# All four ds tiles of a block by DMA transpose, and the plain transfers on GpSimd's queue, from step 160 of an attention backward

## The chip, the cores and the metric

The kernel runs on one core of a Trainium2 chip. The metric is the device time of one execution in microseconds (us); lower is better. The median of the kernel before was 1445.82 us in three runs (1442.79 to 1448.91, a spread of 0.4%) when the prediction was made. The names of the engines in the profile are PE (TensorE), PEld (TensorE's weight loads), DVE (VectorE), ACT (ScalarE), POOL (GpSimd) and SP (SyncE, which here does little but issue DMAs).

## The reference

The kernel computes one transformer block and all its gradients: the output and the gradients of `x`, `wqkv`, `wo` and the three feed-forward weights.

```python
# S = 2048 positions, D = 448, H = 16 heads of 28, F = 1792; bf16 inputs
def attention(x, wqkv, wo):
    q, k, v = split_heads(x @ wqkv)
    p = softmax((q @ k.T) * 28 ** -0.5)
    return merge_heads(p @ v) @ wo

def feed_forward(x, w_gate, w_up, w_down):
    return (silu(x @ w_gate) * (x @ w_up)) @ w_down

def forward(x, ...):
    xn = layernorm(x)
    return x + attention(xn, wqkv, wo) + feed_forward(xn, w_gate, w_up, w_down)

# outputs: forward(...) and its vjp at grad_out
```

The change lies in the backward pass of the attention. For each pair of heads and each pair of a key range and a query range the kernel makes the gradient of the scores, `ds` = (dp product from TensorE) x exp(scores). The gradient of q needs `ds` with keys on the partitions, so every tile of `ds` is transposed into `dsT`.

## The kernel before

The backward has 512 steps. Four steps (`qi` = 0 to 3) are one "block", 128 blocks in all. A step makes one `ds` tile of 128 x 1024 in bf16 (two heads side by side). In a block three tiles are transposed by DMA from SyncE's queue, and the fourth (`qi` = 3) by eight TensorE transposes into PSUM and one ScalarE copy out of it.

```python
def dst_dma(b, ds, qi):
    if qi == 0:
        dsT[b] = bk.tile([P, 4, 2, 4, P], BF16, name="dsT", bufs=3)
    SP.dma_start_transpose(out=dsT[b][:, qi].rearrange("p j kt s -> p (j kt) s"),
                           in_=ds[:].rearrange("p j k -> p (j k)"))

def ew(k):                                   # elementwise work of a step
    ...                                      # ScalarE: exp of the scores into e_sb
        ds = dss[k - 1] = kq.tile([P, 2, 512], BF16, name="ds_sb", bufs=10)
        for j in range(2):
            DVE.tensor_tensor(out=ds[:, j], in0=dps.pop((k - 1, j))[:], in1=est[k - 1][:, j], op=ALU.mult)
        if qi < 2 or qi == 2 and b < NB // 4 - 1:
            ...                              # dst_dma(b, ds, qi)

def tr_unit(b):
    for qi in (3,) if b < NB // 4 - 1 else (2, 3):
        ds = dss.pop(4 * b + qi)
        ps = ps_b.tile([P, 8, P], BF16, name="db", bufs=3)
        for c in range(8):
            PE.transpose(ps[:, c, :], ds[:, c // 4, (c % 4) * P:(c % 4 + 1) * P], ident_bf[:])
        o = dsT[b][:, qi].rearrange("p j kt s -> p (j kt) s")
        ...                                  # qi 2: VectorE copies
            ACTE.copy(out=o, in_=ps[:])      # qi 3
```

`dq_unit(b)` is the reader: 16 matmuls on `dsT`, about nine steps after the block's last `ds`. Beside this, the kernel brings in the data of later work in plain DMA loads of 0.25 to 0.5 MB. A rate rule spreads them over the steps ("drip"), and they go out from SyncE's queue, between the transposes. Results are stored from GpSimd's queue (`store`).

```python
def drop():                                  # called once a step
    ...
    while slow and credit > 0:
        _, _, o, i = slow.pop(0)
        SP.dma_start(out=o, in_=i)
        credit -= size(o)

def load_dx(ch, fq):                         # the largest stream of loads: dau_c, 14 of the 31 MB after step 160
    ...
    d = dxs["pool"].tile([P, 5, 2, 512], BF16, name="dau_c")
    drip(("dx", ch, fq), [(d[:, i - f0:min(i + 2, f1) - f0], F_d[ch, :, i:min(i + 2, f1), 1:3, :]) for i in range(f0, f1, 2)], now + 16)
```

The softmax here doesn't subtract the row's maximum and nothing guards it: scores larger than these inputs give would overflow.

Of the kernel before, what the change touches and what calls it, by code (L numbers as in the profile page):

```python
# [11 lines left out]
FP32 = mybir.dt.float32  # L12
# [91 lines left out]
def kernel(  # L104
# [23 lines left out]
    PE, DVE, ACTE, POOL, SP = nc.tensor, nc.vector, nc.scalar, nc.gpsimd, nc.sync  # L128
# [419 lines left out]
    for i in range(len(chain) + LEAD):  # L548
# [4 lines left out]
        k = i - LEAD  # L553
        if k >= 0:
            b = chain[k]
# [98 lines left out]
    for t in range(4):  # L654
        run(T_unit(xnT, xn_t, t, t % 2 == 0, ps_s if t < 2 else None))
    DVE.tensor_reduce(out=r_ones[:],
                      in_=ident_f[:].rearrange("p (a b) -> p a b", b=HP)[:, :, 28:30],
# [11 lines left out]
    for c in range(3):  # L669
        k = 4 * c  # L670
# [72 lines left out]
    now = 0  # L743
# [13 lines left out]
    def drop():  # L757
        nonlocal credit
        if not slow:
            credit = 0  # L760
            return
        rate, cum = RATE, 0
        for due, _, o, _ in slow:
            cum += size(o)
            rate = max(rate, (cum - credit) / max(due - now - 3, 1))
        credit += rate
        while slow and credit > 0:
            _, _, o, i = slow.pop(0)
            SP.dma_start(out=o, in_=i)
            credit -= size(o)  # L770

    def have(*keys):
        for x in [x for x in slow if x[1] in keys]:
            slow.remove(x)
            SP.dma_start(out=x[2], in_=x[3])

    def load_q(g, qc):
        t = new_q(g, qc)
# [8 lines left out]
    NB = len(steps)  # L787
    dqT, dkv, acc, dsT = {}, {}, {}, {}
    est, dss, sps, dps = {}, {}, {}, {}
# [32 lines left out]
                dps[k - 1, j] = d_ps  # L822

    bk, pend = None, []

    def dst_dma(b, ds, qi):
        if qi == 0:
# [4 lines left out]
    def ew(k):  # L832
        if k < NB:
            est[k] = kq.tile([P, 2, 512], BF16, name="e_sb", bufs=5)
            for j in range(2):
                ACTE.activation(out=est[k][:, j], in_=sps.pop((k, j))[:], func=ACT.Exp, scale=SCALE)  # L836
        if 1 <= k <= NB:
            g, hp, kc, qc, qi = steps[k - 1]
            b = (k - 1) // 4
            ds = dss[k - 1] = kq.tile([P, 2, 512], BF16, name="ds_sb", bufs=10)  # L840
            for j in range(2):
                DVE.tensor_tensor(out=ds[:, j], in0=dps.pop((k - 1, j))[:], in1=est[k - 1][:, j], op=ALU.mult)  # L842
            if qi < 2 or qi == 2 and b < NB // 4 - 1:
                if bk is None:
                    pend.append(lambda: dst_dma(b, ds, qi))
                else:
                    dst_dma(b, ds, qi)
# [9 lines left out]
    k = n = 0  # L857
# [10 lines left out]
    bk = bwd.enter_context(tc.tile_pool(name="bk", bufs=2, reuse_waits="tile"))  # L868
# [7 lines left out]
    def late_dw(c):  # L876
# [10 lines left out]
            store(o[d0:d0 + dn, F - P:], w2[:dn, c, a])  # L887
        yield 110

    dq_acc = bk.tile([P, S // 2], FP32, name="dq_acc", bufs=1)  # L890

    def tr_unit(b):
        for qi in (3,) if b < NB // 4 - 1 else (2, 3):
            ds = dss.pop(4 * b + qi)
            ps = ps_b.tile([P, 8, P], BF16, name="db", bufs=3)
            for c in range(8):
                PE.transpose(ps[:, c, :], ds[:, c // 4, (c % 4) * P:(c % 4 + 1) * P], ident_bf[:])  # L897
            o = dsT[b][:, qi].rearrange("p j kt s -> p (j kt) s")
            if qi == 2:
                DVE.tensor_copy(out=o, in_=ps[:])  # L900
            else:
                ACTE.copy(out=o, in_=ps[:])  # L902

    def kv(k):
        g, hp, kc, qc, qi = steps[k]
        first, last = (qc == 0 and qi == 0), (qc == 3 and qi == 3)
        if first:
            acc[0] = ps_g.tile([P, 512], FP32, name="acc")
        a = acc[0]
        e = est.pop(k)  # L910
        ds = dss[k] if qi == 3 or k == NB - 2 else dss.pop(k)
        sp4 = qside[g, qc][:, 2:4, qi * P:(qi + 1) * P]
        for j in range(2):
            r = HP * pv(2 * hp + j)
            PE.matmul(a[r:r + HP, :], lhsT=sp4[:, 1, r:r + HP], rhs=e[:, j, :],  # L915
                      start=first, stop=last, tile_position=(0, r), skip_group_check=True)
        for j in range(2):
            r = HP * (2 * hp + j)
            PE.matmul(a[r:r + HP, :], lhsT=sp4[:, 0, r:r + HP], rhs=ds[:, j, :],  # L919
                      start=first, stop=last, tile_position=(0, r), skip_group_check=True)  # L920
        if last:
            if kc == 0:
                need(lambda: g == 0 or (g - 1, hp + 1, 1) in s_done)
                dkv[g, hp] = bk.tile([P, S], BF16, name=f"dkv{hp}", bufs=1)
            ACTE.activation(out=dkv[g, hp][:, kc * 512:(kc + 1) * 512], in_=a[:], func=ACT.Copy,
                            scale=(sc_a if hp == 0 else sc_b)[:, 0:1])
            if g < G - 1:
                ksl = slice(kc * 512, (kc + 1) * 512)
                store(dqkvT_d[3 * g + 1 + hp, :, ksl], dkv[g, hp][:, ksl])
            if kc == 3:  # L930
                if g < G - 1:
                    push(*[(480, lambda t8=t8: dsp_unit(g, hp + 1, t8)) for t8 in range(2)])
                elif hp == 0:
                    push(*[(480, lambda t8=t8: dsp_unit(g, hp + 1, t8)) for t8 in range(2)])

    def dq_unit(b):
        g, hp, kc, qc, _ = steps[4 * b]
        t = dsT.pop(b)
        ks = kside[g, kc][:, 2, :].rearrange("p (t r) -> p t r", r=P)
        ps = ps_g.tile([P, 512], FP32, name="genb")  # L940
        for kt in range(4):
            for par in range(2):
                for j in range(2):
                    r = HP * (2 * par + j)
                    h = HP * (2 * hp + j)
                    PE.matmul(ps[r:r + HP, :256], lhsT=ks[:, kt, h:h + HP], rhs=t[:, par::2, j, kt, :],  # L946
                              start=(kt == 0), stop=(kt == 3), tile_position=(0, r), skip_group_check=True)
        qsl = slice(qc * 256, (qc + 1) * 256)
        if kc == 0:
            ACTE.mul(out=dq_acc[:, qsl], in_=ps[:, :256], mul=SCALE)  # L950
            return
        if kc == 3 and hp == 0 and qc == 0:
            dqT[g] = bk.tile([P, 2, S // 2], BF16, name="dqT", bufs=1)
        if kc == 3 and g == G - 1:
            DVE.scalar_tensor_tensor(out=dqT[g][:, hp, qsl], in0=ps[:, :256], scalar=SCALE, in1=dq_acc[:, qsl],  # L955
                                     op0=ALU.mult, op1=ALU.add)
            return
        st = bk.tile([P, 256], FP32, name="dq_st", bufs=1)
        ACTE.mul(out=st[:], in_=ps[:, :256], mul=SCALE)  # L959
        if kc < 3:  # L960
            POOL.tensor_tensor(out=dq_acc[:, qsl], in0=dq_acc[:, qsl], in1=st[:], op=ALU.add)  # L961
            return
        POOL.tensor_tensor(out=dqT[g][:, hp, qsl], in0=dq_acc[:, qsl], in1=st[:], op=ALU.add)
        if qc == 3:
            dst = dqkvT_d[3 * g].rearrange("r (a q s) -> r a q s", q=2, s=P)
            for par in range(2):
                store(dst[64 * hp:64 * hp + 64, :, par],
                      dqT[g][64 * par:64 * par + 64, hp].rearrange("r (a s) -> r a s", s=P))
            if hp == 1:
                stream[3:3] = [(480, lambda hp=hp: dsq_unit(g, hp)) for hp in range(2)]  # L970
                at = [i for i, u in enumerate(stream) if u[1] in (dx_open, tail_open)]
                at = max(at[0] + 1, 5) if at and g != 1 else 5
                s_done.add((g, "w"))
                stream[at:at] = [(2590, lambda c=c: dwq_unit(g, c)) for c in range(4)]

    def dsq_unit(g, hp, tag="genb"):
        ps = (ps_b if tag == "rest" else ps_g).tile([P, 8, P], BF16, name=tag, bufs=2 if tag == "rest" else 1)
        for j in range(8):
            PE.transpose(ps[:, j, :], dqT[g][:, hp, j * P:(j + 1) * P], ident_bf[:])
            if j < 7:  # L980
                yield 60
        DVE.tensor_copy(out=dsp[g][:, :, 0, 64 * hp:64 * hp + 64],
                        in_=ps[:].rearrange("p a (q x) -> p (a q) x", q=2))
        yield 60


    dsp = {}

    def dsp_unit(g, kind, t8, tag="genb"):
# [6 lines left out]
        for j in range(8):  # L996
            t = 8 * t8 + j
            PE.transpose(ps[:, j, :], src[:, t * P:(t + 1) * P], ident_bf[:])
            if j < 7:
                yield 60  # L1000
        (ACTE.copy if tag == "rest" and t8 else DVE.tensor_copy)(out=dsp[g][:, 8 * t8:8 * t8 + 8, kind, :], in_=ps[:])
        s_done.add((g, kind, t8))
        yield 60

# [2 lines left out]
    def dwq_unit(g, c, tag="genb"):  # L1007
# [6 lines left out]
                yield 162  # L1014
        o = bk.tile([P, 3, 4, DH], BF16, name="dwq_o")
        p4 = ps[:].rearrange("p (k h r) -> p k h r", k=3, r=HP)
        cp = ACTE.copy if tag == "rest" else DVE.tensor_copy
        cp(out=o[:dn, 0], in_=p4[:dn, 0, :, :DH])
        cp(out=o[:dn, 1:3, 0:2, :], in_=p4[:dn, 1, :, :DH].rearrange("p (k h) r -> p k h r", k=2))
        cp(out=o[:dn, 2, 2:4, :], in_=p4[:dn, 2, 0:2, :DH])  # L1020
# [364 lines left out]
```

## Time and profile before

| kernel before | value | from |
|---|---|---|
| span of the profiled run, granted clock | 1440.1 us, 0.985 | spans by core |
| TensorE, VectorE, ScalarE busy, whole span | 92%, 80%, 88% | overview |
| block 40 to block 120, from the first `ds` of each | 486.3 us, 6.08 us a block | starts in the trace |
| in those 80 blocks: TensorE, VectorE, ScalarE busy | 467, 443, 446 us | records of the trace |
| SyncE inside DMA issues in the same 80 blocks | 433 us | records of the trace |
| plain traffic in the 80 blocks: SyncE's queue, GpSimd's queue | 30.8 MB, 4.4 MB | packet records |

The table is to be read against the 486 us: TensorE is at 96% of them, and of the others SyncE has the most left, 11%. An engine's busy share doesn't say which resource sets the pace here. The lines of the views are in the prediction below.

### The profile page before, as it was taken

To read this page: it belongs to the slowest core of one execution; us is meant where nothing else is said; L and a number is where in the kernel's file an instruction comes from. 1 tells how busy PE (TensorE), PEld (TensorE's weight loads), DVE (VectorE), ACT (ScalarE), POOL (GpSimd) and SP (SyncE) were. 2 spreads that over 40 slices of the span, in tenths; PEclk is the share of its full clock that TensorE was granted. 3 is DMA by queue.
4 is the path that set the end of the run, shared out by engine and by line. 5 is a ranking of instruction groups with operands and counts; after the bars stand their busy time and mean duration, and the time that the engine had idled before them with its cause. 6 is when DMAs were issued, how large, how long until landed. Compare 5 with 4: busy or idle time off the path is not lost. (4 is left out here: it accounts for less than half of the span.)

```text
span 1440.1 us, 34682 instructions
## 1 busy us (share of the span) xinstructions
PE 1326.3 (92%) x12647; PEld 541.0 (38%) x12708; DVE 1151.8 (80%) x1997; ACT 1261.5 (88%) x2193; POOL 403.6 (28%) x561
## 2 busy tenths in 40 slices
PE   5889999999999999889999999999999999999996
PEld 2333333333333333333333434433443444444343
DVE  6667757666676676578998998888889999989988
ACT  5789988988889999869989989899989999989974
POOL 6464524464334454111112112201111011010006
PEclk9999999999999999989999999999999999999998
DMA  5796956796678586799999999999999999999971
GB/s 154 181 199 165 235 122 160 187 195 164 146 162 192 147 172 145 178 234 226 226 213 217 232 220 188 196 209 229 228 173 194 209 223 230 201 191 203 198 142 60
DMA packets 681179, 271.69 MB, mean 189 GB/s; under 512 B 606424, under 2 KB 655824, under 8 KB 681008
## 3 DMA queue, kind: packets, MB, share of 16 engines
q1 hardware_dynamic: 672576, 255.35, 87.1%
q0 software_dynamic: 7024, 13.82, 4.1%
q8 instruction: 100, 1.64, 0.5%
q14 instruction: 71, 0.58, 0.1%
q10 hardware_dynamic: 1408, 0.30, 0.1%
HBM read 65.09 MB, written 60.36 MB: 87 GB/s over the span
## 5 line engine op out<-in xcount | busy, mean ns | idle before, releaser
L842 DVE TENSOR_TENSOR ds_sb<-db,e_sb 128x512 bf16<-128x512 f32 x1024 | 646.8, 684 | 51.3 <-issue 21.1
L836 ACT ACTIVATE e_sb<-sb 128x512 bf16<-128x512 f32 x1024 | 554.8, 611 | 60.4 <-PE db L820 44.5
L612 ACT ACTIVATE eT<-s_w 128x1024 bf16<-128x1024 f32 x256 | 263.5, 1029 | 46.1 <-PE s_ps L609 43.1
L614 ACT ACTIVATE eT<-s_ps 128x512 bf16<-128x512 f32 x512 | 280.4, 612 | 0.0
L820 PE MATMUL db<-kd,qd 32*128 32x512 bf16 x1024 | 234.4, 384 | 8.2 <-DVE ds_sb L842 7.4
L812 PE MATMUL sb<-kd,qd 32*128 32x512 bf16 x1024 | 210.4, 387 | 5.1 <-DMA qd<-QD_d 3.3
L961 POOL TENSOR_TENSOR dq_acc<-dq_acc,dq_st 128x256 f32<-128x256 f32 x64 | 46.2, 721 | 455.4 <-ACT dq_st L959 455.4
L919 PE MATMUL acc<-ds_sb,qd 128*32 128x512 bf16 x1024 | 161.0, 391 | 0.0
L915 PE MATMUL acc<-e_sb,qd 128*32 128x512 bf16 x1024 | 158.8, 391 | 1.3 <-DVE dw_o L528 1.3
L902 ACT COPY dsT<-db 128x1024 bf16<-128x1024 bf16 x128 | 130.1, 1016 | 14.6 <-PE db L897 13.9
L380 POOL TENSOR_TENSOR nn<-nn,ag 128x512 f32<-128x512 f32 x56 | 71.2, 1271 | 252.2 <-DVE ag L378 243.7
L609 PE MATMUL s_ps<-QQ,KK 32*128 32x512 bf16 x512 | 125.4, 385 | 3.9
L1128 PE MATMUL genb<-wguT,dau_c 128*128 128x448 bf16 x448 | 117.5, 355 | 6.3 <-ACT dq_st L959 3.9
L609 PE MATMUL s_w<-QQ,KK 32*128 32x512 bf16 x512 | 100.3, 387 | 13.1 <-ACT eT L612 10.4
L812 PEld LDWEIGHTS <-qd 32*128 32x128 bf16 x1024 | 48.2, 91 | 149.4 <-issue 140.3
L421 PE MATMUL gen<-xn_t,f_sp 128*128 128x448 bf16 x416 | 91.8, 354 | 2.6 <-DVE nn L395 1.7
L421 PEld LDWEIGHTS <-f_sp 128*128 128x128 bf16 x640 | 55.7, 98 | 75.0 <-issue 31.9
L946 PE MATMUL genb<-dsT,kd 128*32 128x256 bf16 x2048 | 79.5, 275 | 1.9 <-DVE dqT L955 0.6
L897 PE MATMUL db<-ident_bf,ds_sb 128*128 128x128 bf16 x1032 | 79.4, 220 | 1.1 <-DVE ds_sb L842 1.1
L897 PEld LDWEIGHTS <-ds_sb 128*128 128x128 bf16 x1032 | 68.3, 99 | 24.1 <-issue 5.3
L451 PE MATMUL gen<-eT,VS 128*32 128x512 bf16 x1024 | 68.4, 384 | 5.5 <-DVE nn L395 3.3
L381 POOL TENSOR_TENSOR nn<-nn,tt 128x512 f32<-128x512 f32 x56 | 72.0, 1286 | 4.4
(167 smaller groups left out, 1911.0 us busy)
## 6 DMA issues: line engine op xcount, KB each, us to landing
F_d<-hda SPq DMA_DIRECT2D x56, 384.0 KB, 3.1
dau_c<-F_d SPq DMA_DIRECT2D x24, 512.0 KB, 4.4
qd<-QD_d SPq DMA_DIRECT2D x16, 512.0 KB
kd<-KD_d SPq DMA_DIRECT2D x16, 384.0 KB, 4.0
dsT<-ds_sb SPq DMA_TRANSPOSE x383, 4.3
dc<-dqkvT_d SPq DMA_DIRECT2D x12, 384.0 KB, 3.9
h_c<-F_d SPq DMA_DIRECT2D x8, 512.0 KB, 4.4
wT_d<-wT_f SPq DMA_DIRECT2D x14, 256.0 KB, 3.6
```

The lines of the kernel that those rows point to most:

```text
L421: PE.matmul(ps[:, :D], lhsT=fsp[fc][:, t // 4, w, t % 4, :], rhs=rhs[:, t, :], start=(t == 0), stop=(t == NT - 1))
L609: PE.matmul(sp4[hh], lhsT=KK[g][r:r + HP, kt * P:(kt + 1) * P], rhs=QQ[g][r:r + HP, qsl], start=True, stop=True, tile_position=(r, 0))
L612: ACTE.activation(out=e2[0][:], in_=wide[:], func=ACT.Exp, scale=SCALE)
L614: ACTE.activation(out=e2[1][:, j], in_=sp4[2 + j], func=ACT.Exp, scale=SCALE)
L812: PE.matmul(s_ps[:], lhsT=qside[g, qc][r:r + HP, 0, qi * P:(qi + 1) * P], rhs=kside[g, kc][r:r + HP, 0, :], start=True, stop=True, tile_po ...
L820: PE.matmul(d_ps[:], lhsT=qside[g, qc][r:r + HP, 1, qi * P:(qi + 1) * P], rhs=kside[g, kc][r:r + HP, 1, :], start=True, stop=True, tile_po ...
L836: ACTE.activation(out=est[k][:, j], in_=sps.pop((k, j))[:], func=ACT.Exp, scale=SCALE)
L842: DVE.tensor_tensor(out=ds[:, j], in0=dps.pop((k - 1, j))[:], in1=est[k - 1][:, j], op=ALU.mult)
L897: PE.transpose(ps[:, c, :], ds[:, c // 4, (c % 4) * P:(c % 4 + 1) * P], ident_bf[:])
L902: ACTE.copy(out=o, in_=ps[:])
L915: PE.matmul(a[r:r + HP, :], lhsT=sp4[:, 1, r:r + HP], rhs=e[:, j, :], start=first, stop=last, tile_position=(0, r), skip_group_check=True)
L919: PE.matmul(a[r:r + HP, :], lhsT=sp4[:, 0, r:r + HP], rhs=ds[:, j, :], start=first, stop=last, tile_position=(0, r), skip_group_check=True)
```

## The change

The intent is to free TensorE of eight transposes a block and ScalarE of one copy, by sending the fourth tile by DMA as well from block 40 (step 160) on. Because SyncE's queue was nearly full, the plain transfers move from there to GpSimd's queue at the same step, and ScalarE takes over copies of the projection gradients (`dwq`) and of their transposed inputs (`dsp`) from VectorE. A one-element copy on GpSimd (`tie`) keeps its transfers in step with the work.

```diff
-            SP.dma_start(out=o, in_=i)
+            (SP if now < 160 else POOL).dma_start(out=o, in_=i)          # in drop(); the same in have()
...
+    PB = 40
+    def by_pe(b):
+        return (3,) if b < PB else (2, 3) if b == NB // 4 - 1 else ()
...
-            if qi < 2 or qi == 2 and b < NB // 4 - 1:
+            if qi not in by_pe(b):                                       # in ew(): by DMA
...
-        for qi in (3,) if b < NB // 4 - 1 else (2, 3):
+        for qi in by_pe(b):                                              # in tr_unit(): by TensorE
...
+            if now >= 160:
+                POOL.tensor_copy(out=tie[:], in_=dq_acc[0:1, qsl.start:qsl.start + 1])
...
-        DVE.tensor_copy(out=dsp[g][:, :, 0, 64 * hp:64 * hp + 64],
+        (DVE.tensor_copy if tag == "rest" or now < 4 * PB else ACTE.copy)(out=dsp[g][:, :, 0, 64 * hp:64 * hp + 64],
...
-        cp = ACTE.copy if tag == "rest" else DVE.tensor_copy
+        cp = ACTE.copy if tag == "rest" or now >= 4 * PB else DVE.tensor_copy   # dwq; another dsp copy likewise
```

More of the change, by code (lines that the diff above doesn't have):

```diff
@@ L774, in have @@
             slow.remove(x)
-            SP.dma_start(out=x[2], in_=x[3])
+            (SP if now < 160 else POOL).dma_start(out=x[2], in_=x[3])
     def load_q(g, qc):
@@ L888, in late_dw @@
         yield 110
+    tie = bk.tile([1, 1], FP32, name="tie", bufs=1)
     dq_acc = bk.tile([P, S // 2], FP32, name="dq_acc", bufs=1)
     def tr_unit(b):
-        for qi in (3,) if b < NB // 4 - 1 else (2, 3):
+        for qi in by_pe(b):
             ds = dss.pop(4 * b + qi)
@@ L910, in kv @@
         e = est.pop(k)
-        ds = dss[k] if qi == 3 or k == NB - 2 else dss.pop(k)
+        ds = dss[k] if qi in by_pe(k // 4) else dss.pop(k)
         sp4 = qside[g, qc][:, 2:4, qi * P:(qi + 1) * P]
@@ L1000, in dsp_unit @@
                 yield 60
-        (ACTE.copy if tag == "rest" and t8 else DVE.tensor_copy)(out=dsp[g][:, 8 * t8:8 * t8 + 8, kind, :], in_=ps[:])
+        (ACTE.copy if (t8 if tag == "rest" else now >= 4 * PB) else DVE.tensor_copy)(out=dsp[g][:, 8 * t8:8 * t8 + 8, kind, :], in_=ps[:])
         s_done.add((g, kind, t8))
```

## The prediction

> **What bounds the kernel now.** I read the overview first, then the time by stretch, the costliest groups, the timelines of single engines, and last the DMA queue's own records.
>
> The overview (each digit is a 36 us slice) shows where the change acts. Slices 18 to 39 are the attention backward: 512 steps, four to a "block", 128 blocks. The change acts from step 160 (block 40), which begins near 880 us. There TensorE, VectorE, ScalarE and the DMA engines are all in their last tenth, so no share names the bound.
>
> ```profile
> PE   5889999999999999889999999999999999999996
> ...
> DVE  6667757666676676578998998888889999989988
> ACT  5789988988889999869989989899989999989974
> ...
> DMA  5796956796678586799999999999999999999971
> ```
>
> The same by stretch, blocks before and after step 160. Columns: length, busy us (instructions) of each engine, granted clock, DMA share, GB/s.
>
> ```profile
> core 0: us, PE busy (x) PEld busy (x) DVE busy (x) ACT busy (x) POOL busy (x), PEclk, DMA share, GB/s
> 640.00:880.00 240.00, 224.78 (x2571) 94.53 (x2571) 219.05 (x356) 218.74 (x406) 38.71 (x62) 0.99 1.16 221
> 885.00:1390.00 505.00, 485.44 (x5569) 205.01 (x5571) 461.08 (x782) 464.09 (x867) 63.95 (x95) 0.99 1.08 203
> ```
>
> In 505 us VectorE idles 44 and ScalarE 41: that is all a lighter ScalarE can win from them. A DMA share over 1 only means that packets overlap in flight.
>
> The groups that the change touches, from the page (count, busy us, mean ns):
>
> ```profile
> L842 DVE TENSOR_TENSOR ds_sb<-db,e_sb 128x512 bf16<-128x512 f32 x1024 | 646.8, 684 | 51.3 <-issue 21.1
> ...
> L902 ACT COPY dsT<-db 128x1024 bf16<-128x1024 bf16 x128 | 130.1, 1016 | 14.6 <-PE db L897 13.9
> ...
> L897 PE MATMUL db<-ident_bf,ds_sb 128*128 128x128 bf16 x1032 | 79.4, 220 | 1.1 <-DVE ds_sb L842 1.1
> ```
>
> The block's length comes from the starts of its dq matmuls: block 40 at 881.1 us, block 120 at 1366.8, so 485.7 / 80 = 6.07 us. VectorE needs 8 x 0.62 = 5.0 us of it for ds (0.62 is the spacing back to back; the 684 ns overlap), ScalarE 8 x 0.515 + 0.93 + 0.32 = 5.4 us for exp, the transposed copy and dq, plus fillers on both.
>
> The view that decides is SyncE's queue, which issues the DMA transposes. The tile view gives minimum, median and maximum of one issue in ns, the timeline how closely they stand:
>
> ```profile
> L829 SPq DMA_TRANSPOSE dsT<-ds_sb x383: 1231/1296/4112, 623.7 to 1392.5; - x192
> ...
> 641.18 4.49 SPq L829 DMA_TRANSPOSE dsT<-ds_sb  x3
> 645.73 0.57 SPq L769 DMA_DIRECT2D wd_sb<-in_B_w_down_dram  x1
> 646.39 4.72 SPq L829 DMA_TRANSPOSE dsT<-ds_sb  x2
> 651.17 0.57 SPq L769 DMA_DIRECT2D h_c<-F_d  x1
> 651.83 5.29 SPq L829 DMA_TRANSPOSE dsT<-ds_sb  x3
> 657.18 0.57 SPq L769 DMA_DIRECT2D h_c<-F_d  x1
> 657.85 4.24 SPq L829 DMA_TRANSPOSE dsT<-ds_sb  x2
> 662.14 0.58 SPq L769 DMA_DIRECT2D x_c<-in_A_x_dram  x1
> 662.82 4.45 SPq L829 DMA_TRANSPOSE dsT<-ds_sb  x3
> ```
>
> Between 641 and 667 us the queue never rests: with three transposes a block and heavy loads SyncE is already full. A transpose costs it 1.29 us and 0.09 us to the next start, **1.38 us**. The 13 in these 26.1 us take 17.9; the other 8.2 go to four loads of 1.79 MB together: 0.67 each for the issue, and 5.5 us in which transposes stand behind their bytes, 3.1 us per MB. A least-squares fit over every nine successive issues from 650 to 882 us (issue times against the DMA packets in each stretch) gives 1.39 us a transpose, 0.59 a plain issue, 1.9 us per MB of plain bytes on SyncE's own queue, and **5.1 us per MB** of the stores that GpSimd issues (90% interval 3.5 to 6.2).
>
> **What the Trainium skill says.**
> - "DMA: Bandwidth & Descriptors", section "Issuing engines are not separate DMA queues": DMAs from all issuers run on the same 16 engines and interleave; another issuer saves only sequencer time. The trace agrees: GpSimd's few stores slow SyncE's transposes.
> - Same page, section "Queues, rings and completion order": an engine takes turns between queues packet by packet. The packet records agree and add a cost: during GpSimd's 0.36 MB of stores near 833 us, transpose packets fall from 11 per 10 ns to 1 to 7, with gaps in which hardly any packet starts.
> - "SBUF — State Buffer", section "Summary: rules for kernel authors": GpSimd's descriptor writing is starved while VectorE runs a 2x or 4x mode. No such wait is visible in this trace; VectorE's main operation reads PSUM.
> - "ScalarE: Activation LUTs", section "What ACT_TABLE_LOAD costs": 186 ns + 0.833 ns per element, so 1039 ns for 1024; the transposed copy takes 1016.
>
> **The change part by part**, for the 87 blocks 40 to 126 (block 127 keeps its two TensorE transposes).
> 1. Removed: 87 x 8 = 696 transposes on TensorE. At 79.4 us / 1032 = 77 ns this is 54 us of its time, 0.6 a block. Also 87 ScalarE copies, 0.93 us each in marginal time: 81 us. This also frees a db bank in PSUM.
> 2. Moved from VectorE to ScalarE: 14 dsp copies and 48 small dwq copies (the instruction order confirms both counts). They cost VectorE 8.8 + 8.4 = 17 us; on ScalarE, at about 1 us and 0.25 us, 14 + 12 = 26. ScalarE falls by about 55 us net, VectorE by 17, to about 5.5 us a block with its fillers: VectorE would be the bound of the compute engines. With the 44 us of idle time mostly kept, these two parts alone are worth 20 to 45 us.
> 3. Added: 87 transposes on SyncE. Its floor becomes 4 x 1.38 = **5.52 us** a block, without a stall.
> 4. Moved: 78 plain loads (the count in the instruction order), about 31 MB or 0.36 MB a block, from SyncE to GpSimd. This saves SyncE 0.9 x 0.67 = 0.6 us a block, but not the bytes' hold on the 16 engines. GpSimd has time: 64 us busy of 505, and an issue is 0.56 us there.
> 5. The 20 one-element "tie" copies only pace GpSimd; I count nothing for them.
>
> SyncE's queue then sets the block: 5.52 us plus what 0.36 + 0.05 MB (loads and stores) of GpSimd traffic takes from the transposes. At 1.9 us per MB this is 0.8, at 5.1 it is 2.1. I choose 2.4 us per MB, **1.0 us**: the 5.1 comes from small stores whose switching cost weighs more per byte than that of loads of 0.25 to 0.5 MB. So 6.5 us a block against 6.07: +0.45 x 87 = +39 us, 1446 + 39 = **1485 us**. Four tiles of slack (dq of a block comes nine steps after its last ds) turn short stalls into nothing but do not help against a queue that is too slow on average.
>
> **Rivals.**
> - *The intent comes true.* When only transposes run, the packet records show 1024 of them done in 0.91 us, faster than SyncE issues (1.38): a third of the DMA time is left, 1.8 us a block, and 0.41 MB at the 390 GB/s seen over 5 us needs 1.05. If two queues share so smoothly, SyncE stays at its floor, the block is 5.5 to 5.75 us and VectorE almost binds beside it: -28 to -48 us, about 1400 to 1418. For it: the sum fits. Against it: the collapse of the transpose rate around GpSimd's traffic.
> - *It is a wash.* The gain of parts 1 and 2 and the loss of parts 3 and 4 cancel: blocks of 5.8 to 6.35 us, 1422 to 1470. For it: the queue in between absorbs about one transpose (the first after a plain load issues in 1237 ns, the second in about 2000).
> - *Stores are typical of loads.* At 5.1 us per MB the block is 7.6 us: +130 us, 1580.
> - *GpSimd becomes a wait.* dq_st has one buffer, so ScalarE waits for GpSimd's add; a load ahead of it in GpSimd's order that waits for a free buffer would hold ScalarE. Buffers are mostly released by work that stands earlier in the program, so I expect little.
>
> **Range and chances.** Between the smooth sharing and nearly the stores' rate: 1410 to 1570. Faster by over 2% (under 1417) needs blocks under 5.74 us, only 0.2 over SyncE's floor: 0.12. Within 2%, blocks up to about 6.4: 0.30. Slower: 0.58.
>
> **What would show it.** Right: SyncE's queue without rest after 900 us, a transpose issue's median still near 1.29 us but its mean well over 1.4, transposes issued ever later after their ds, TensorE waiting for dsT at the dq matmuls, VectorE and ScalarE with far more than 44 us idle, lower GB/s. Wrong: blocks near 5.6 us with VectorE 95% busy (smooth sharing), or waits of ScalarE at dq_st for GpSimd, or of TensorE for qd, kd or dau_c that arrive late (a GpSimd order problem, not a DMA one). Nothing before 880 us may move by more than a few us.

## The result, and the profile after

The changed kernel is correct. Its median is 1580.61 us in four runs (1563.91 to 1589.96), against 1445.22 us (1442.79 to 1448.91, four runs) of the kernel before on the same chip. Every ratio in this document is the mean time of one kernel's fast runs over the mean time of the other's fast runs of the same rounds, so it isn't quite the ratio of the medians. Here it is 1.0896, 95% interval 1.0803 to 1.0989: **9% slower**. The profiled run was the longest of the four (1589.96 us). It is 1.66% above the fastest of its kernel and counts as slow for that. Its clock, 0.934, lies just under those of the others (0.935 to 0.947), so its picture may be read, but its sizes are up to 1.7% (26 us) large, and nothing below may rest on them alone.

The overview of the changed kernel (slices of 39.7 us; the change begins in slice 22):

```profile
PE   6899999999999998999999778866988867968875
DVE  6766666656676675889999667745877756858867
ACT  5889899898999986989998667755866655757753
PEclk9999999999999998999999998887988978988998
DMA  5988677766786767999999999999999999999991
```

All three compute engines get idle at slice 22 and stay uneven to the end. One row remains full, the DMA engines, and it was full in the kernel before too (a full row doesn't prove a bound: the share counts overlapping packets and goes over 1). PEclk, the granted clock of TensorE, dips with it: the Trainium skill, "TensorE: Matmul & The Clock Gate", section "Part 1: The HAM clock gate", has the clock halved after about 3.4 us of idling, and TensorE now has waits of up to 7 us. The trace agrees in part: from 885 to 1530 us the clock stood at half in 24 stretches, 150 us in all (mean 0.88, below), and the first of them begins at 903.9 us, 4.5 us into a wait of 7.1 us. But only nine waits there were longer than 3.4 us. What the slower clock adds to the loss wasn't tested.

The same by stretch, blocks before and after step 160 (columns as in the prediction):

```profile
640.00:880.00 240.00, 226.25 (x2555) 93.66 (x2551) 217.21 (x353) 216.83 (x402) 38.50 (x63) 0.97 1.15 218
885.00:1530.00 645.00, 517.43 (x4943) 178.19 (x4943) 450.76 (x728) 421.26 (x851) 118.98 (x195) 0.88 1.13 193
```

Up to 880 us little moved (block 40 begins 3 us later). After it VectorE does its 451 us of work in 645 us, so 194 us are idle, where the kernel before had 44. ScalarE's and VectorE's work did shrink as predicted (in blocks 40 to 119 to 404 and 428 us, from 446 and 443). The granted clock is 0.88 instead of 0.99, and the DMA engines move 193 GB/s instead of 203, although more of the stretch is spent on them.

What the engines now wait for, first in the costliest groups (idle time ahead of the group, and what ended most of it), then in the list of waits from 885 to 1530 us (total us, times, longest):

```profile
L846 DVE TENSOR_TENSOR ds_sb<-db,e_sb 128x512 bf16<-128x512 f32 x1024 | 648.1, 685 | 213.7 <-DMA dsT<-ds_sb 81.2
...
L951 PE MATMUL genb<-dsT,kd 128*32 128x256 bf16 x2048 | 99.0, 294 | 74.0 <-DMA dsT<-ds_sb 65.5
```

```profile
DVE ds_sb L846 <- DMA dsT<-ds_sb: 79.4, 32, 7.4
...
ACT dq_st L966 <- PE genb L951: 63.9, 39, 7.6
PE genb L951 <- DMA dsT<-ds_sb: 60.2, 41, 7.1
```

VectorE waits for a DMA transpose before it may write: the ten `ds_sb` buffers are all held by tiles whose transpose has not been read yet. TensorE waits for `dsT` at the dq matmuls, and ScalarE waits for those. The group of VectorE's `ds` idled 51.3 us in the kernel before and the waits for DMA transposes there came to 3.4 us (VectorE) and less than 0.3 us (dq matmuls).

SyncE's queue, in the tile view (minimum, median, maximum ns of one issue) and in a piece of its timeline:

```profile
L833 SPq DMA_TRANSPOSE dsT<-ds_sb x470: 1231/1306/7661, 625.4 to 1538.7; - x157
```

```profile
997.04 35.26 SPq L833 DMA_TRANSPOSE dsT<-ds_sb  x19
```

GpSimd's timeline around it, in which the loads are issued that used to stand in SyncE's queue:

```profile
1003.37 1.41 POOL L769 DMA_DIRECT2D dau_c<-F_d  x2
1009.25 0.72 POOL L968 TENSOR_TENSOR dq_acc<-dq_acc,dq_st 128x256 f32<-128x256 f32 x1 [4.48 <-ACT dq_st L966]
1009.92 0.56 POOL L769 DMA_DIRECT2D dau_c<-F_d  x1
```

In 35.26 us SyncE gets 19 transposes out without one plain DMA between them, 1.86 us each. The median issue is that of the kernel before (1306 ns against 1296), but the longest is 7661 ns. The packet records show what happens in those: in the 2 us before the two `dau_c` loads (0.5 MB each) arrive, about 113 transpose packets of 256 bytes start in every 100 ns, which is a whole tile in 0.91 us. From 1005.2 to 1009.4 us it is mostly 0 to 13 in 100 ns, while up to fourteen of the loads' packets of 4096 bytes start. A stretch worth four transposes does less than one.

The fit of the prediction, made over the changed kernel (nine successive issues, 905 to 1500 us), gives 1.42 us a transpose and **4.6 us per MB** of GpSimd's traffic (90% interval 3.8 to 5.5). The split between the two isn't that firm: the same fit gives about 1.5 us and 3 us per MB over e12 below, which moves the same bytes, and 1.5 and 3.9 over e4. In blocks 40 to 119 a transpose is now issued 10.2 us after its `ds` in the median (6.5 to 15.9 in the middle 80%), where it was 1.3 us (0.1 to 3.3). Block 40 to block 120 takes 617.5 us, 7.72 a block, against 486.3, so 131 of the 148 us between the two profiled runs are lost in those blocks.

### The profile page after: what moved, and what is told of

It reads as the page before. It is cut to its first block, busy times and chain, and to the rows that moved or that the text cites. A ratio compares the mean times of both kernels' runs of the same rounds, so it can differ in the third digit from the quotient of the medians.

```text
span 1588.2 us, 33298 instructions
## 1 busy us (share of the span) xinstructions
PE 1367.9 (86%) x12012; PEld 512.9 (32%) x12012; DVE 1137.4 (72%) x1935; ACT 1212.6 (76%) x2168; POOL 458.9 (29%) x659
## 5 line engine op out<-in xcount | busy, mean ns | idle before, releaser
L820 PE MATMUL db<-kd,qd 32*128 32x512 bf16 x1024 | 251.2, 407 | 55.8 <-DVE ds_sb L846 55.1
L812 PE MATMUL sb<-kd,qd 32*128 32x512 bf16 x1024 | 220.8, 409 | 4.8 <-DMA qd<-QD_d 3.3
L924 PE MATMUL acc<-ds_sb,qd 128*32 128x512 bf16 x1024 | 171.9, 413 | 0.3 <-DVE ds_sb L846 0.2
L920 PE MATMUL acc<-e_sb,qd 128*32 128x512 bf16 x1024 | 169.4, 414 | 1.3 <-DVE dw_o L528 1.3
L951 PE MATMUL genb<-dsT,kd 128*32 128x256 bf16 x2048 | 99.0, 294 | 74.0 <-DMA dsT<-ds_sb 65.5
L1135 PE MATMUL genb<-wguT,dau_c 128*128 128x448 bf16 x448 | 122.7, 389 | 2.0 <-ACT dq_st L966 1.2
L951 PEld LDWEIGHTS <-kd 128*32 128x32 bf16 x2048 | 61.5, 101 | 126.8 <-issue 77.5
L966 ACT ACTIVATE dq_st<-genb 128x256 f32<-128x256 f32 x88 | 34.7, 394 | 67.1 <-PE genb L951 67.1
L1135 PEld LDWEIGHTS <-dau_c 128*128 128x128 bf16 x448 | 38.1, 103 | 97.2 <-issue 81.5
```

The source lines that it names most:

```text
L812: PE.matmul(s_ps[:], lhsT=qside[g, qc][r:r + HP, 0, qi * P:(qi + 1) * P], rhs=kside[g, kc][r:r + HP, 0, :], start=True, stop=True, tile_po ...
L820: PE.matmul(d_ps[:], lhsT=qside[g, qc][r:r + HP, 1, qi * P:(qi + 1) * P], rhs=kside[g, kc][r:r + HP, 1, :], start=True, stop=True, tile_po ...
L920: PE.matmul(a[r:r + HP, :], lhsT=sp4[:, 1, r:r + HP], rhs=e[:, j, :], start=first, stop=last, tile_position=(0, r), skip_group_check=True)
L924: PE.matmul(a[r:r + HP, :], lhsT=sp4[:, 0, r:r + HP], rhs=ds[:, j, :], start=first, stop=last, tile_position=(0, r), skip_group_check=True)
L951: PE.matmul(ps[r:r + HP, :256], lhsT=ks[:, kt, h:h + HP], rhs=t[:, par::2, j, kt, :], start=(kt == 0), stop=(kt == 3), tile_position=(0, r ...
L1135: PE.matmul(ps[:, :D], lhsT=d[:, i // 2, i % 2, tsl], rhs=dxs["w", fq][:, i // 2, i % 2, :], start=(i == 0), stop=(i == n - 1))
```

## The experiments

Two theories stand after this. **A:** DMA time is the budget. A block must get its transposes and the plain bytes of its time through SyncE's queue and the 16 DMA engines, and both the fourth tile and the megabytes on GpSimd's queue overdraw it. **B:** the fault lies in one part, and the rest is sound: either GpSimd (its loads come late, or its copies and the `tie` hold others up), or ScalarE (too full for the copies given to it). Fourteen kernels were run. Figures in brackets after a time are its lowest and highest run; the letters of theories in an expectation are those that it defines itself. The kernel before had medians of 1440 to 1445 us in the different rounds, so kernels of different rounds are better compared by their ratios. e4 and e8 are wrong on purpose in one output, all others are correct. All the profiles of the experiments are of fast runs.

### e1_loads_only: the plain transfers alone on GpSimd

```diff
 def by_pe(b):
-    return (3,) if b < PB else (2, 3) if b == NB // 4 - 1 else ()
+    return (2, 3) if b == NB // 4 - 1 else (3,)     # three DMA tiles, as before
 # dsp and dwq copies stay on VectorE; loads from GpSimd and the tie as in the changed kernel
```

> Only the plain transfers move to GpSimd from step 160; the fourth ds tile stays with TensorE and ScalarE, the projection copies stay on VectorE. Theory A (GpSimd's packets hold up the transposes on the 16 shared DMA engines, 4.7 us per MB of SyncE's time, against about 2 us per MB plus 0.6 us an issue for the same loads on SyncE's own queue): SyncE needs 3 x 1.40 + 0.41 MB x 4.7 = 6.1 us a block, about the present 6.07, so 1445 to 1475 us, SyncE's queue without rest. Theory B (it is the fourth transpose alone that overloads SyncE, and the queue of the loads is indifferent): SyncE is relieved of 0.6 us a block, 1435 to 1447 us. Theory C (loads arrive late or GpSimd's order holds ScalarE): 1500 us or more, with waits for qd, kd, dau_c or of dq_st for GpSimd.

Measured: 1482.92 us (1480.32 to 1485.27), ratio 1.026 (1.0242 to 1.0279). This is worse than its theories A and B said, and better than its C. Moving the loads out of SyncE's queue, with nothing added to it, costs 38 us. So theory B's form "the loads on GpSimd are free and only the fourth tile hurts" falls, and theory A had it too cheap: a block of 3 x 1.42 + 0.44 MB x 4.6 = 6.3 us was to be expected at the fitted rate, and 6.51 was measured in the profile.

### e2_tiles_only: four tiles by DMA, loads left on SyncE

```diff
 # relative to the changed kernel
-            (SP if now < 160 else POOL).dma_start(out=o, in_=i)
+            SP.dma_start(out=o, in_=i)              # and no tie
```

> Only the fourth transpose and the copies on ScalarE; all plain transfers stay on SyncE's queue. Theory A: 4 x 1.40 + 0.9 x 0.59 + 0.36 MB x 2 + 0.05 x 4.8 = 7.1 us a block, (7.1 - 6.07) x 87 = +90 us, about 1535 us, less than the changed kernel's 1580 by what the loads cost less on SyncE's queue. Theory B (the fourth transpose is all of it): 1580 or more, since SyncE also issues the loads. Theory C (GpSimd's part is all of it): 1400 to 1450.

Measured: 1544.51 us (1543.73 to 1547.58), ratio 1.0691 (1.0673 to 1.0708), as theory A said. The loss of the two parts adds up: 38 us for the loads (e1) and 99 for the tiles with the copies (e2) make 137, and the changed kernel loses 135. So there is no single guilty part.

### e3_act_queue: the plain transfers on ScalarE's queue

```diff
-            (SP if now < 160 else POOL).dma_start(out=o, in_=i)
+            (SP if now < 160 else ACTE).dma_start(out=o, in_=i)
```

> The changed kernel with the plain transfers from step 160 issued by ScalarE's hardware queue in place of GpSimd's software one. If any second queue that takes turns with the transposes holds them up (A1): 1550 to 1600 us. If it is GpSimd's software descriptors (A2): the loads cost about 2 us per MB, 4 x 1.40 + 0.36 x 2 + 0.05 x 4.8 = 6.6 us a block, about 1490 us. ScalarE's own issue time is at most 0.6 us a block of the 1.2 us that it has idle.

Measured: 1544.24 us (1530.09 to 1546.41), ratio 1.0654 (1.0598 to 1.0709): between the two, and equal to e2. A second queue for the same bytes gives nothing, and it is 36 us better than GpSimd's queue by the medians (35 by the fast runs, give or take 16). The `tie` is still in this kernel, so as a copy it isn't what costs; what it does to the times at which GpSimd sends its loads was not tested.

### e4_fewer_bytes: dau_c loaded once

```diff
     def load_dx(ch, fq):
         ...
+        if (ch, fq) != (0, 0):
+            dxs[ch, fq] = dxs[0, 0]
+            return
```

> The changed kernel with the gradient chunks dau_c loaded once and used again (a wrong out_1 on purpose): about 14 MB of the 31 MB of loads on GpSimd are gone, transposes and arithmetic stay. Theory A: 0.41 to 0.25 MB a block at 4.7 us per MB, 0.75 us x 87 = 65 us less than the changed kernel, about 1515 us. Theory B: no change, 1580 us.

Measured: 1522.64 us (1518.67 to 1540.35), ratio 1.0559 (1.0496 to 1.0622). From block 40 to 120, 13.4 MB fewer go through GpSimd's queue, and the profiled time of these blocks falls by 63 us (617.5 to 554.4), 4.7 us per MB. But the 617.5 is of the slow run. By the fast runs alone the ratios differ by 0.034, which is 49 us or 3.6 us per MB, with an interval of about 2.4 to 4.8. The bytes cost what the fit says within this width; 4.6 itself isn't confirmed.

### e5_copies_only: the dsp and dwq copies alone on ScalarE

```diff
 # relative to the kernel before
-        cp = ACTE.copy if tag == "rest" else DVE.tensor_copy
+        cp = ACTE.copy if tag == "rest" or now >= 4 * PB else DVE.tensor_copy   # and the dsp copies likewise
```

> The kernel before with only the dsp and dwq copies moved from VectorE to ScalarE from step 160. Theory A (the loss of 135 us comes from SyncE's transposes and the bytes beside them; the copies have no part in it): within 1% of the kernel before, 1438 to 1455 us, ScalarE some 26 us busier and VectorE some 17 us less. Rival B (ScalarE is so near to its limit, 446 of 486 us busy in blocks 40 to 119 of the kernel before, that 26 us more make it the bound): 1460 to 1475 us, with VectorE and TensorE waiting for ScalarE's e_sb and dq_st.

Measured: 1449.13 us (1444.64 to 1454.97), ratio 1.0058 (1.0026 to 1.009). The table by stretch of this kernel, to be held against the second line of the kernel before in the prediction:

```profile
885.00:1390.00 505.00, 478.44 (x5512) 202.33 (x5508) 442.26 (x714) 477.53 (x923) 63.87 (x95) 1.00 1.07 202
```

The two windows don't hold the same work; over the whole span ScalarE is busy 18 us more (1279.3 against 1261.5) and VectorE 15 less. The 62 copies take the predicted 26 us on ScalarE in sum (14 of about 1.04 us, 48 of about 0.24), but part of that overlaps with their neighbours. The kernel loses about 8 us. That is small, but it is no gain: this part alone makes nothing faster.

### e6_pairs: two tiles in one transpose

A cheaper way to issue was the next thought: if a transpose has a fixed part, two neighbouring tiles in one transpose of 128 x 2048 save one of them. In the forward of the kernel before, the fastest of such large transposes had gone in 1.56 us, but not all (minimum, median, maximum ns):

```profile
L200 SPq DMA_TRANSPOSE qk_sp<-KK x4: 1564/1688/2619, 47.2 to 415.3; - x4
L200 SPq DMA_TRANSPOSE qk_sp<-QQ x4: 1931/3027/3211, 60.1 to 450.6; - x4
```

```diff
 # relative to e2_tiles_only
-            ds = dss[k - 1] = kq.tile([P, 2, 512], BF16, name="ds_sb", bufs=10)
+            if qi % 2 == 0:
+                pair[0] = kq.tile([P, 2, 2, 512], BF16, name="ds_sb", bufs=5)
+            ds = dss[k - 1] = pair[0][:, qi % 2]
...
-        SP.dma_start_transpose(out=dsT[b][:, qi]..., in_=ds[:]...)
+        SP.dma_start_transpose(out=dsT[b][:, q0:q0 + qn].rearrange("p q j kt s -> p (q j kt) s"),
+                               in_=ds.rearrange("p q j k -> p (q j k)"))   # once both tiles are there
```

> Four DMA tiles a block with the plain loads on SyncE, as in e2_tiles_only, but two tiles of ds lie side by side and go in one 128x2048 transpose instead of two of 128x1024 (blocks 0 to 39: one pair and one single). Theory P (a DMA transpose holds SyncE for a fixed part of about 1.1 us plus little per column; in the kernel before the fastest qk_sp transposes of 128x2048 took 1.56 to 1.74 us against 1.24 to 1.29 for 128x1024, and the packets of a pair alone need 2 x 0.91 us): 2 x 1.9 + 0.55 for the plain issues + 0.77 for their 0.385 MB + 0.28 for GpSimd's stores = 5.4 us of SyncE a block, so SyncE is no longer the bound; 1385 to 1445 us, at or below the kernel before. Rival Q (the time goes by size: a pair costs 2 x 1.38): 1535 to 1555 us as e2_tiles_only. Rival R (waiting for the second tile of a pair makes dsT late): more than 1450 us with SyncE idle.

Measured: 1518.52 us (1514.7 to 1522.84), ratio 1.0536 (1.0509 to 1.0562). The tile view of this kernel:

```profile
L833 SPq DMA_TRANSPOSE dsT<-ds_sb x255: 1231/3071/5529, 626.6 to 1467.4; - x128
```

A miss for the theory that was to give 1385 to 1445 us. A pair holds SyncE for 3.07 us in the median (3.14 in blocks 40 to 119, where all are pairs), more than two singles. The packet records say when. The 44 pairs during whose issue no plain packet started took 2.04 us in the median, close to theory P's 1.9 and less than two singles in the same state (1.29 us each in e2, though their packets need only 0.91). The 61 pairs beside more than 0.3 MB of plain bytes took 3.48 us, and singles beside as much 2.13 (e2). So the issue of a single tile has a floor of its own, and plain bytes make both forms longer; what theory P left out is that a pair pays more for them. In the profiles e6 gains 20 us on e2 in blocks 40 to 119. 17 of them are fewer gaps between issues (the time in which SyncE is in no DMA issue falls from 37 to 20 us), so SyncE's own time isn't free in this queue.

### e7_pairs_gpsimd: the changed kernel in pairs

> The changed kernel (plain transfers on GpSimd) with its transposes in pairs of 128x2048. Theory P with the 4.6 us per MB of GpSimd traffic: 2 x 1.9 + 0.444 MB x 4.6 = 5.8 us of SyncE a block, so 1420 to 1470 us, slower than e6_pairs by 20 to 40. Rival Q: 1560 to 1590 us as the changed kernel. Rival S (the loads on GpSimd delay the work by their own lateness, not through SyncE): still above 1500 us, with waits for dau_c, qd or kd in place of those for dsT.

The edit is e6's, made in the changed kernel. Measured: 1556.49 us (1549.29 to 1580.88), ratio 1.0783 (1.0741 to 1.0826), 24 us better than without pairs by the medians, 16 by the fast runs (the intervals touch), and far from what theory P said. One of its four runs was slow. By the fast runs it lies 36 us above e6 of the same rounds, with an interval of about 7 us: the same price for GpSimd's queue that e3 showed, 1.2 us per MB more.

### e8_fewer_syncq: e2 with dau_c loaded once

> e2_tiles_only (four tiles by DMA, plain loads on SyncE) with dau_c loaded once and used again: wrong result on purpose, 26 loads and 13.4 MB fewer. Theory A (on SyncE's own queue a plain load costs 0.59 us an issue and 2 us per MB): 15 + 27 = 42 us less than e2_tiles_only, about 1500 us. Rival B (bytes cost the same 4.6 us per MB on any queue): 77 us less, about 1467 us. Rival C (on the own queue only the issues count): 15 us less, about 1530 us.

The edit is e4's, made in e2. Measured: 1502.55 us (1496.3 to 1503.0), ratio 1.0412 (1.0379 to 1.0445), 42 us less than e2 by the medians, 40 by the ratios. Theory A had just this number; its split into issues and bytes is tested by e14. For 13.4 MB it is 3.0 us per MB by the fast runs (about 2.6 to 3.4) and 3.1 in the profiles (575.0 to 533.6 us). The same loads over GpSimd's queue gave 3.6 by the fast runs and 4.7 by the profiles (e4).

### e9_every_2nd and e10_every_4th: a dose of DMA tiles

```diff
 # relative to the kernel before; n = 2 (e9) or 4 (e10)
+    def by_pe(b):
+        return (2, 3) if b == NB // 4 - 1 else () if b >= PB and b % n == 0 else (3,)
```

> The kernel before with one thing changed: from block 40 on every second block sends its fourth tile by DMA instead of TensorE and ScalarE (40 more transposes). Theory A (a budget of DMA and SyncE time a block: 5.74 us in the kernel before, of its 6.08; each tile 1.38): 5.74 + 0.69 = 6.43 us, so 28 us more, 1465 to 1480 us. Rival L (no slack in the kernel before: the loss goes in proportion to the tiles, half the 99 us that e2_tiles_only lost with 80): 1485 to 1500 us. Rival G (what fewer TensorE and ScalarE operations give is worth more): below 1441 us.

> As e9_every_2nd in every fourth block (20 more transposes). Theory A: 5.74 + 0.35 = 6.09 us a block, just what the kernel before takes, and TensorE freed of 20 x 8 transposes (12 us): 1432 to 1450 us. Rival L: a quarter of 99 us, about 1466 us. This is the try at a kernel that beats the one before.

Measured: e9 1481.34 us (1476.26 to 1482.72), ratio 1.0264 (1.0245 to 1.0283); e10 1451.08 us (1446.15 to 1455.18), ratio 1.0057 (1.0038 to 1.0075). The kernels have 22, 44 and 87 more tiles by DMA (20, 40 and 80 of them in blocks 40 to 119). The 22 cost 9 us, the 44 39 and the 87 (e2, with the copies that e5 prices at 8) 99. The first 22 cost 0.4 us each, the next 22 1.4, the last 43 1.2 to 1.4: about a transpose each, once the slack is gone. Both lie one us above the range of theory A, and its rivals are further off: proportion would put e10 at 1466, and the rival's range for e9 begins at 1485. There is a little slack in the kernel before, and it is used up before or at 22 tiles, with no gain for the eight TensorE transposes that each of them saves. As a try to beat the kernel before, e10 failed by half a per cent.

### e11_every_4th_pairs: the same in pairs

> e10_every_4th with neighbouring tiles in one 128x2048 transpose. e6_pairs showed 3.07 us for a pair, so no fixed part is saved and only the gaps between issues are (it gained 25 us where SyncE was the bound). Theory A with slack: within 10 us of e10_every_4th, 1425 to 1450 us. Rival R (the pair comes later than its first tile, and later transposes delay the work even where the queue is not full): 10 to 30 us more than e10_every_4th.

Measured: 1446.81 us (1444.4 to 1451.92), ratio 1.0035 (1.0018 to 1.0051), 4 us better than e10 by the medians, though the intervals overlap and blocks 40 to 119 take the same in both profiles (493.6 and 493.1 us). It is still no better than the kernel before. Waiting for the second tile of a pair does no harm.

### e12_small_loads: half-size loads on GpSimd

```diff
 # relative to the changed kernel
-        [(d[:, i - f0:min(i + 2, f1) - f0], F_d[ch, :, i:min(i + 2, f1), 1:3, :]) for i in range(f0, f1, 2)]
+        [(d[:, i - f0], F_d[ch, :, i, 1:3, :]) for i in range(f0, f1)]
```

> The changed kernel with dau_c loaded in pieces of 256 KB instead of 512 KB, the same bytes on GpSimd, 24 DMAs more. Theory A (the cost of GpSimd's transfers is by byte): the same as the changed kernel, 1560 to 1590 us. Rival B (two large loads at once shut the transposes out, in bursts, and that is what costs more than on a hardware queue): 1540 to 1555 us, as on ScalarE's queue. Rival D (a cost for each DMA on GpSimd, 1 us or more): 1605 us or more.

Measured: 1566.45 us (1559.34 to 1579.67), ratio 1.0871 (1.083 to 1.0912) against 1.0896 (1.0803 to 1.0989): the same within about 14 us. A cost of 1 us for each DMA is excluded. Rival B is only made less likely: its range ended at 1555, and in the profile of e12 blocks 40 to 119 take 591 us.

### e13_act_1k and e14_sync_1k: smaller packets

What was left open was why a megabyte costs more over GpSimd's queue. The packet records gave a thought: the same `dau_c` loads move in packets of 4096 bytes from GpSimd's queue (in e12 too) and of 2048 from ScalarE's and SyncE's. If an engine takes turns between queues packet by packet, as the prediction quotes, then large packets take the larger share from transpose packets of 256 bytes. (That one packet record of the trace is one such turn is assumed here; no run shows it.)

```diff
 # relative to e3_act_queue (e13) and e2_tiles_only (e14)
-        [(d[:, i - f0:min(i + 2, f1) - f0], F_d[ch, :, i:min(i + 2, f1), 1:3, :]) for i in range(f0, f1, 2)]
+        [(d[:, i - f0:min(i + 2, f1) - f0, w], F_d[ch, :, i:min(i + 2, f1), 1 + w, :]) for i in range(f0, f1, 2) for w in range(2)]
```

> e3_act_queue (the changed kernel with its plain transfers on ScalarE's hardware queue) with the loads of dau_c cut into rows of 1024 bytes instead of 2048, the same bytes in twice as many DMAs. Theory P (queues take turns packet by packet at each DMA engine, so a transpose beside packets of half the size gets twice as many turns): the transposes go on during loads, and SyncE's transposes are shorter in the mean; 1515 to 1535 us against 1544. Rival B (by byte whatever the packet): 1538 to 1550 us. Rival D (smaller packets move less well, and ScalarE pays for 32 more issues): 1552 us or more.

> e2_tiles_only (plain loads on SyncE, the transposes' own queue) with the same cut of dau_c to rows of 1024 bytes. Nothing takes turns here, so all theories expect the cost of 32 more issues at 0.59 us, 19 us, and perhaps 5 us for smaller packets: 1555 to 1570 us. Under theory P it is then slower than e13_act_1k by 25 us or more; under rival B by about 20; under rival D by less than 10.

Measured: e13 1534.34 us (1532.99 to 1540.96), ratio 1.0645 (1.062 to 1.0671), where e3 has 1.0654 (1.0598 to 1.0709); e14 1542.91 us (1533.77 to 1546.16), ratio 1.0698 (1.0658 to 1.0737), where e2 has 1.0691. The packets were 1024 bytes, as the records show. The median of e13 lies inside the range of theory P (1515 to 1535), but the kernel before ran 5 us faster in these rounds, and by the ratios neither kernel moved. So the size of the packets that take turns is not shown to be the cause: between 1 and 2 KB on ScalarE's queue there is no difference within the intervals, some 0.6%. That 4 KB would differ is neither shown nor excluded. e14 also refutes a term that all theories shared: 32 more issues on SyncE, priced at 0.59 us each, cost nothing clear of noise (1 us, give or take 6). Why plain issues are free here while fewer gaps helped in e6 is not explained.

**What the runs add up to.** One budget for blocks 40 to 119: 1.42 us for each 128 x 1024 tile by DMA (the fit), 3.1 us per MB of plain traffic on a hardware queue (e2 less e8) and 4.6 us per MB on GpSimd's (the fit, from the slow run and so on the high side).

| kernel | DMA tiles | MB on SyncE's / GpSimd's queue | budget, us | measured, us |
|---|---|---|---|---|
| before | 240 | 30.8 / 4.4 | 456 | 486 |
| e10 | 260 | 30.8 / 4.4 | 485 | 493 |
| e9 | 280 | 30.8 / 4.4 | 513 | 521 |
| e1 | 240 | 0 / 35.4 | 504 | 521 |
| e8 | 320 | 17.5 / 4.4 | 529 | 534 |
| e2 | 320 | 30.9 / 4.4 | 570 | 575 |
| e14 | 320 | 30.7 / 4.4 | 570 | 567 |
| e4 | 320 | 0 / 22.1 | 556 | 554 |
| e12 | 320 | 0 / 35.3 | 617 | 591 |
| after (slow run) | 320 | 0 / 35.5 | 618 | 618 |

Measured is the time from the first `ds` of block 40 to that of block 120 in each profile. Where the budget is clearly the longest need (320 tiles) it meets the measurement within 5 us, but for e12. Of these rows e2, e8 and after have lent a constant; e14 and e4 are checks, and e12 is one that fails by 26 us: in that execution GpSimd's traffic cost about 3.9 us per MB beside 1.42 a tile. Near the point where the compute engines need as much (about 486 us), the time lies 8 to 30 us above it, as the plain loads come unevenly and some blocks are short of DMA while others are short of compute.

## Why the prediction was wrong

The direction was right and the size was not: 1485 us was named with a range up to 1570, and 1580.61 was measured. By its own steps:

- **The bound, SyncE's queue of transposes: held.** SyncE's queue ran full, transposes came ever later after their `ds`, and VectorE and TensorE waited for them, all as announced. An issue with no plain packet beside it stayed at 1.29 us in the median (161 of them in the changed kernel); 54 issues beside more than 0.3 MB took 3.14. So what the prediction had too small is how much plain bytes stretch the issues.
- **Two readings that were off.** VectorE's row isn't "in the last tenth": nine of its sixteen digits from slice 24 on are 8. And the 3.1 us per MB between 641 and 667 us divides by the loads issued there (1792 KB); the packets of the stretch are 2.30 MB on SyncE's queue and 0.36 MB on GpSimd's, so 5.5 us are about 2.1 per MB, near the fit's 1.9.
- **Part 1, TensorE and ScalarE freed: happened, worth nothing.** VectorE and ScalarE lost the predicted work and spent the time waiting. e10 shows it apart: 22 blocks freed of eight TensorE transposes each, no gain. The 20 to 45 us that parts 1 and 2 together were to be worth if the queue allowed were never seen.
- **Part 2, the copies: no gain by itself.** e5 put it at 0.6% slower. VectorE's "about 5.5 us a block" is what it had before (443/80); less 17 us it is 5.34, and the changed kernel shows 428/80 = 5.35.
- **Part 3, the floor of 4 x 1.38 = 5.52 us: held.** The fit over the changed kernel gave 1.42, so 5.68 (about 1.5 over e4 and e12, so 6.0).
- **Part 4, the step that failed: "I choose 2.4 us per MB, 1.0 us".** The term was mis-sized. Even on the transposes' own hardware queue a MB costs 3.0 us (e2 against e8), and GpSimd's queue adds 1.2 (e7 against e6), so 4.2; e4 gives 3.6 by the fast runs, the fit over the slow run 4.6. The bytes are 0.444 MB a block, not 0.41. At 4.2 this makes 5.68 + 1.9 = 7.5 us a block, and the fast runs' mean gives 6.07 + 129.5/87 = 7.56. Of the 1.06 us by which that exceeds the 6.5 predicted, about 0.9 is this term and 0.16 the transposes' 0.04 us each; with the other fits' split the transposes' share would be larger. The reason given for the choice, that small stores cost more per byte than large loads, was an argument without a run, against a number that the trace had already given. e4 and e8 contradict it: the bytes that they take away are loads of 0.25 to 0.5 MB, and those cost more than 2.4 us per MB on either queue (on GpSimd's by e4 at the edge of its interval).
- **Part 5, the tie: nothing seen.** It stays in e3, which is as fast as e2. Its pacing of GpSimd's loads was not tested apart.
- **The rivals.** "Stores are typical of loads", 7.6 us a block and 1580 us, came true in its number. That is partly luck: it took 5.1 us per MB of 0.41 MB beside a floor of 5.52, where the runs show about 4.2 of 0.444 MB beside 5.68. "The intent comes true" rested on transposes and loads that share the engines without loss; e3 denied it even for a hardware queue. "GpSimd becomes a wait" didn't come: from 885 to 1530 us the list of waits has none for a load of `dau_c`, `qd` or `kd`, and 0.5 us in all for GpSimd's work (the `tie`), its own orders apart.
- **What stays open.** Why a megabyte over GpSimd's queue costs some 1.2 us more than over a hardware queue (3.0 to 3.3 us). The packet records only tell where it is: from 900 to 1380 us the DMA engines move less than 60 GB/s in 89 us of the changed kernel, in 69 of e3 and in 62 of e2, counted in steps of 100 ns; likewise in 113 of e1 against 82 of the kernel before. Halving the largest loads changed nothing clear of noise (e12), nor did smaller packets on ScalarE's queue (e13), and the `tie` as a copy costs nothing visible (e3). No kernel of the series beat the one before.

## What to carry to other kernels

Before work is moved to DMA, add up the DMA time of the stretch (transposes by their duration in a full queue, plain bytes by a rate that is measured next to transposes) and compare it with the stretch. Moving bytes to another issuer's queue took nothing off this sum (e3, 577 us against 575 of e2), and on GpSimd's it cost 38 us (e1). When the trace has already given a rate for the operation in question, predict with that rate, and let an argument for a milder one widen the range instead of moving its centre.

## What the Trainium skill lacked or had wrong

- "DMA: Bandwidth & Descriptors", section "Issuing engines are not separate DMA queues", is right that the issuers share the engines, but gives no price. Beside a stream of DMA transposes, plain loads cost 3.0 to 3.1 us per MB on the transposes' own queue (e2 against e8), about 3.3 on ScalarE's (e3: 577 us for the 80 blocks, less 454 for the tiles and 20 for the stores, over 30.9 MB) and about 4.2 on GpSimd's (1.2 more, e7 against e6; 3.6 to 4.7 by e4). The page has the hardware queues as generally faster, but no cost per byte beside transposes.
- "Advanced Engine Details and Errata", section "X-Bar Transpose (TRN2)", says that transposes are as fast as regular DMAs and expects 350 to 400 GB/s. Here a tile of 262,144 bytes took 0.91 us in the best bursts (288 GB/s) and, issued one by one in a full queue, 1.42 us (185 GB/s).
- No page says how long the issue of a transpose holds SyncE on this chip: 1.29 us in the median with no plain packet beside it and 2.13 beside more than 0.3 MB (e2, 128 x 1024); 2.04 and 3.48 for 128 x 2048 (e6).
- No page mentions that a full stream of transposes pauses. From 900 to 1380 us the kernels have 24 to 36 stretches of 1.0 us or more in which less than 60 GB/s move; in e8 there are 28 (1.0 to 1.7 us, 38 us in all), often about 14 us apart. The packet records show what they go with: all 28 begin within 1 us of a packet of 16,384 bytes on the queue that the profile calls "q8 instruction", and 28 of its 33 packets are followed by one (26 of 30 pauses in the kernel before). With the packets' times shifted by 5 us, none of the 28 has one. No run changed these transfers, so that they are the cause isn't shown.
